# The Fourier transform along the channels on twice folded rows, in a fused linear attention and Fourier FFN kernel

## The chip, the cores and the metric

One NeuronCore of a Trainium2 chip. The metric is device time in microseconds of one execution. The kernel before took 1024.85 us, the median of 3 runs (1022.36 to 1027.26).

## What is computed

```python
# q, k, v: (8, 8, 576, 64); g_norm: (64)
kv = einsum('bhsd,bhse->bhde', k, v)
out = einsum('bhsd,bhde->bhse', q, kv)
rms = sqrt(mean(out * out, axis=-1, keepdims=True) + 1e-06)
x = (out / rms * g_norm)            # heads side by side: x is (8, 576, 512)
X = fft(fft(x, axis=1), axis=2)     # along the sequence, then along the channels
u = x + real(X)
un = (u - mean(u)) / sqrt(var(u) + 1e-06)
return u + maximum(un @ w_ch1, 0) @ w_ch2    # w_ch1: (512, 2048), w_ch2: (2048, 512)
```

w_ch1 and w_ch2 come as float64, and the kernel converts them itself.

## The kernel before, in words

**Number format.** Transforms and FFN run in fp32r. Each operand is split in a rounded high part and a low part, and each product is three matmuls (`passes`: high x high, high x low, low x high).

**First part, batch by batch (8 batches).** `plan_kv` (L574) makes k'v for a pair of heads; `plan_q` (L643) transposes q on TensorE; `plan_out` (L669) multiplies. A batch's 576 rows are handled as three tiles of 96 or 97 partitions, each holding a row p of the first half beside its mirror row of the second half, 512 channels each. `plan_y` and `plan_fold` scale x and fold it. Because the input is real, only sums (for the cosine) and differences (for the sine) of mirrored entries are needed, along the sequence and along the channels: L785 (VectorE) adds each channel d to channel 512 - d, for d = 1 to 256, taking the mirror row for the second term; L792 (GpSimd) then makes sum and difference of the two rows. ScalarE (L798) and GpSimd (L801) split the result `xe` into `xh` and `xl`. Column 0 has no partner; L779 (ScalarE) puts it into `x0`, and its own small transform (L1131) gives a constant per row that is added much later.

`plan_seq` transforms along the sequence: for each part (0 cosine, 1 sine) and each chunk `ch` of 128 folded channels, 9 matmuls of 290 columns (L816) make one bank `ps_f`, which ScalarE (L830) and VectorE (L834) split into the two tiles `pt`. `plan_chn` transforms along the channels: for each of the three row tiles and each part, 2 chunks x 3 passes = 6 matmuls with 96 or 97 weight columns (a slice of `pt`) and 258 moving columns of the table `cd` (L851). A ScalarE copy (L863) and two VectorE operations (L871) combine the two parts, and two additions (L883, L886; VectorE in batch 0, GpSimd later) add the result to x. `plan_turn` transposes the rows (L942) and splits them into `unTh` and `unTl` (L951, L954), blocks of 512 tokens for the FFN.

**FFN.** `ffn1` (L424) and `ffn2` (L442) take 512 moving columns each. Of the 16 slices of the hidden layer, 3 are done on a block as soon as it is complete (`plan_early`), between the batches' work; the others come after the first part, in `segs`, while the last weights are converted on VectorE (L359 to L369, L986, L995; later L1220).

**What sets the order.** `Plan` collects operations with an engine, a cost, a rank (batch and stage) and buffer rings, and plays them through: at each moment every engine takes the ready operation of lowest rank whose buffers are free. The order found is the program's order on each engine, fixed up to 95 us of the plan's clock (`PIN_UNTIL`). The table `SHIFT` moves the rank of single stages of single batches. FFN work has ranks over 1000 and so fills gaps. `plan_spare` gives TensorE 45 pairs of matmuls on a constant tile (`ps_s`, L494) of still higher rank, as filler. In batch 0 the DFT tables are loaded and split by `plan_dft` (L514 to L520).

## Time and profile before

| | |
|---|---|
| median of 3 runs | 1024.85 us |
| the profiled execution / its span | 1022.79 us / 1021.0 us |
| TensorE busy | 1002.3 us, 6070 matmuls |
| VectorE, ScalarE, GpSimd busy | 475.3, 324.8, 314.4 us |
| L851, the channel transform | 288 matmuls, 37.8 us busy |
| L816, the sequence transform | 288 matmuls |
| `ps_s`, filler | 90 matmuls |

The lines of the profile read `line engine operation out<-in shapes xcount | busy us, mean ns of one | idle before it, and what ended that`. Matmuls overlap, so the mean of one (285 ns for L851) is longer than the distance between two; distances are taken from windows and from the timeline. An fp32 matmul appears as two records, an fp32r matmul as one. PEld is TensorE's weight load.

### The profile page before, as it was taken

To read this page: it belongs to the slowest core of one execution; us is meant where nothing else is said; L and a number is where in the kernel's file an instruction comes from. 1 tells how busy PE (TensorE), PEld (TensorE's weight loads), DVE (VectorE), ACT (ScalarE), POOL (GpSimd) and SP (SyncE) were. 2 spreads that over 40 slices of the span, in tenths; PEclk is the share of its full clock that TensorE was granted. 3 is DMA by queue.
4 is the path that set the end of the run, shared out by engine and by line. 5 is a ranking of instruction groups with operands and counts; after the bars stand their busy time and mean duration, and the time that the engine had idled before them with its cause. 6 is when DMAs were issued, how large, how long until landed. Compare 5 with 4: busy or idle time off the path is not lost.

```text
span 1021.0 us, 15425 instructions
## 1 busy us (share of the span) xinstructions
PE 1002.3 (98%) x6070; PEld 844.0 (83%) x6070; DVE 475.3 (47%) x847; ACT 324.8 (32%) x657; POOL 314.4 (31%) x328
## 2 busy tenths in 40 slices
PE   5999999999999999999999999999999999999997
PEld 5898888889888888888888888888888888888886
DVE  4897656654788879997131313131221311311211
ACT  2666556554644434344221202121121120210110
POOL 0526768775675132235722303020020010100000
PEclk9999999999999999999999999999999999999999
DMA  9989778664346775645553514230320400400101
GB/s 250 212 230 282 181 209 258 162 170 131 137 163 213 268 253 191 236 129 170 161 179 86 180 59 150 82 125 0 141 67 1 165 21 1 165 0 1 42 1 42
DMA packets 109260, 140.74 MB, mean 138 GB/s; under 512 B 51854, under 2 KB 76482, under 8 KB 104580
## 3 DMA queue, kind: packets, MB, share of 16 engines
q1 hardware_dynamic: 105652, 132.28, 41.9%
q0 software_dynamic: 1920, 6.29, 1.9%
q10 hardware_dynamic: 1616, 1.18, 0.5%
q8 instruction: 48, 0.79, 0.3%
q14 instruction: 24, 0.20, 0.1%
HBM read 88.33 MB, written 51.40 MB: 137 GB/s over the span
## 4 chain that ended last, share of the span: by engine, by line
PE 97%; DMA 1%; ACT 0%; POOL 0%; DVE 0%; issue 0%; SPq 0%; DVEq 0%; POOLq 0%
PE ps_h L424 38%; PE acc L442 38%; PE ps_o L669 4%; PE ps_f L816 4%; PE ps_f L851 4%; PE ps_k L574 3%; PE ps_s L494 2%; PE ps_q L643 2%; PE ps_t L942 2%; DMA qt<-in_q_dram 1%; PE ps_w L383 1%; DMA vm<-in_v_dram 0%; POOL x L883 0%; ACT x L686 0%; DVE uu L1324 0%
## 5 line engine op out<-in xcount | busy, mean ns | idle before, releaser
L424 PE MATMUL ps_h<-unTh,w 128*128 128x512 f32 x1152 | 356.6, 391 | 1.2 <-ACT fq L647 1.2
L442 PE MATMUL acc<-w,hh 128*128 128x512 f32 x1152 | 345.5, 390 | 0.0
L437 DVE SCALAR_TENSOR_TENSOR hl<-ps_h,hh 128x512 fp32r<-128x512 f32 x144 | 99.1, 688 | 371.8 <-ACT hh L434 367.5
L442 PEld LDWEIGHTS acc<-w,hh 128*128 128x128 f32 x1152 | 215.1, 188 | 44.3
L424 PEld LDWEIGHTS ps_h<-unTh,w 128*128 128x128 f32 x1152 | 214.8, 188 | 44.8 <-ACT fq L647 1.4
L434 ACT ACTIVATE hh<-ps_h 128x512 fp32r<-128x512 f32 x144 | 85.8, 596 | 454.0 <-PE ps_h L424 439.2
L424 PE MATMUL ps_h<-unTl,w 128*128 128x512 f32 x576 | 224.3, 389 | 0.0
L442 PE MATMUL acc<-w,hl 128*128 128x512 f32 x576 | 213.5, 389 | 0.0
L424 PEld LDWEIGHTS ps_h<-unTl,w 128*128 128x128 f32 x576 | 108.1, 188 | 22.6
L442 PEld LDWEIGHTS acc<-w,hl 128*128 128x128 f32 x576 | 108.1, 188 | 22.6
L1271 POOL DMA_INDIRECT uu<-u_scr,rowidx x24 | 23.2, 968 | 285.1 <-DVE uu L1324 177.9
L709 POOL TENSOR_TENSOR x<-x,gb 96x512 f32<-96x512 f32 (+1 forms) x42 | 55.0, 1330 | 45.7 <-ACT x L686 40.3
L1290 POOL TENSOR_TENSOR uu<-uu,up 128x512 f32<-128x512 f32 x36 | 45.7, 1298 | 45.2 <-ACT up L1287 45.2
L1234 POOL TENSOR_TENSOR w<-wap,w 128x512 fp32r<-128x512 f32 x18 | 26.4, 1467 | 75.3 <-ACT w L1233 69.1
L669 PEld LDWEIGHTS ps_o<-kvt,fq 64*96 64x96 f32 (+1 forms) x864 | 40.9, 162 | 5.7 <-issue 4.0
L1324 DVE SCALAR_TENSOR_TENSOR uu<-acc,rs_yb,uu 128x512 f32<-128x512 f32 x36 | 25.2, 744 | 42.5 <-PE acc L442 42.5
L669 PE MATMUL ps_o<-kvt,fq 64*96 64x64 f32 (+1 forms) x864 | 44.4, 248 | 0.0
L696 DVE TENSOR_REDUCE ss<-ps_o 96x8 f32<-96x512 f32 (+1 forms) x48 | 32.0, 682 | 26.5 <-ACT ps_o L691 26.3
L792 POOL TENSOR_TENSOR xe<-ab 96x256 f32<-96x256 f32 (+1 forms) x46 | 38.0, 845 | 18.7 <-DVE ab L785 17.9
L816 PE MATMUL ps_f<-cs,xh 96*128 96x290 f32 (+1 forms) x192 | 39.0, 300 | 0.0
L1278 DVE BATCH_NORM_STATS2 bst<-uu 128x6 f32<-128x512 f32 x36 | 24.5, 687 | 29.0 <-DMA uu<-u_scr,rowidx 19.8
L851 PE MATMUL ps_f<-cd,pt 128*96 128x258 f32 (+1 forms) x288 | 37.8, 285 | 0.0
(114 smaller groups left out, 1022.4 us busy)
## 6 DMA issues: line engine op xcount, KB each, us to landing
raw<-in_moe_w_ch_dram SPq DMA_DIRECT2D x32, 512.0 KB
unT_scr<-unTh SPq DMA_DIRECT2D x9, 1024.0 KB
unT_scr<-unTl SPq DMA_DIRECT2D x9, 1024.0 KB
part_scr<-part SPq DMA_DIRECT2D x36, 256.0 KB
unTh<-unT_scr SPq DMA_DIRECT2D x9, 1024.0 KB
unTl<-unT_scr SPq DMA_DIRECT2D x9, 1024.0 KB
up<-part_scr SPq DMA_DIRECT2D x36, 256.0 KB
out_dram<-uu SPq DMA_DIRECT2D x36, 256.0 KB
```

What stands on the lines that cost most here:

```text
L424: nc.tensor.matmul(ps, w[c][:, kc * P : (kc + 1) * P], unT[a][:, kc, :], start=(idx == 0), stop=(idx == 3 * KC - 1),)
L434: nc.scalar.activation(hh, ps, AF.Relu)
L437: nc.vector.scalar_tensor_tensor(hl, ps, 0.0, hh.bitcast(F32), ALU.max, ALU.subtract)
L442: nc.tensor.matmul(acc, hpair[a][:, i * P : (i + 1) * P], w[c], start=(first and n == 0), stop=(last and n == 2),)
L574: nc.tensor.matmul(ps.t[s * D : (s + 1) * D, pr * D : (pr + 1) * D], km[:, s, j, :] if j < 4 else kr[:, h, :], vm[:, s, j, :] if j < 4 els ...
L669: nc.tensor.matmul(pss[s].t[:n, at : at + D], fqs[side].t[half, m, :n], kvt.t[half, m], start=True, stop=True,)
L696: nc.vector.tensor_reduce(ss.t[0][:n, :, t, s::2], pss[s].t[:n].rearrange("p (u m e) -> p u m e", u=2, e=D), AX.X, ALU.add,)
L709: nc.gpsimd.tensor_tensor(v_, v_, gb[:n].unsqueeze(1).to_broadcast([n, H, D]), ALU.mult)
L792: nc.gpsimd.tensor_tensor(o[:, s], a[:, 0], a[:, 1], ALU.subtract if s else ALU.add)
L816: nc.tensor.matmul(ps.t[:, :NS], xs[t].t[a][:n, part, ch * P : (ch + 1) * P], cs[:n, part, c, t, :], start=(idx == 0), stop=(idx == 8),)
L851: nc.tensor.matmul(ps.t[:n, :ND], pt.t[a][:, part, ch, offs[t] : offs[t] + n], cd[:, part, c, ch, :], start=(idx == 0), stop=(idx == 5),)
L1290: nc.gpsimd.tensor_tensor(us[j][i], us[j][i], part, ALU.add)
```

## The change

The spectrum along the channels has a symmetry that the kernel before did not use: with d' = 256 - d, cos(2 pi d' k / 512) is cos(2 pi d k / 512) for even k and its negative for odd k; for the sine it is the other way round. So after the sequence transform the two chunks of 128 channels are added and subtracted (row d with row 256 - d), and even columns k need only one of the results and odd columns the other. Each matmul of `plan_chn` still contracts 128 rows, but has 130 moving columns (even or odd ones) instead of 258; their number stays.

For this, `plan_fold` writes the second chunk in reverse order (three VectorE instructions instead of one). `plan_seq` handles both chunks of a part together: ScalarE copies the second bank to a new tile `far`, VectorE writes the sum into the second bank and the difference into the first, and both are split as before. Channel 128 is its own partner, and channel 256 is partner of column 0: in the cosine part the vector `paired` (1, and 0 for the last row) keeps them apart, one table row gets 1 in its odd columns, and the constant of column 256 goes into that of column 0, which a VectorE reduction (L834 of the new kernel) now adds instead of ScalarE. `plan_chn` writes even columns beside odd ones in a bank; copy and mix read them interleaved. The table's load and split are half as long (`plan_dft_d`).

The diff, cut:

```diff
 SHIFT = {
-    ("", "POOL", 20): 18,
-    ("chn", "ACT", -34): 54.5,
...
+    ("", "POOL", 30): 16.5,
+    ("chn", "DVE", -34): 14.5,
...
+    "x": 8, "raw": 2, "e2": 4, "wk": 2, "xhl": 3, "pt": 1, "two": 2, "far": 1,
...
+    NE = DH // 2 + 2
...
-    cd = cst.tile([P, 2, 2, 2, ND], F32R, name="cd")
+    cd = cst.tile([P, 2, 2, 2, NE], F32R, name="cd")
+    paired = cst.tile([P, 1], F32, name="paired")
+    nc.vector.tensor_scalar(paired, ident[:, P - 1 : P], -1.0, 1.0, ALU.mult, ALU.add)
...
+    def plan_dft_d(part, r):
+        raw = ring("x", one, [P, 2 * DM], "draw")
+        pad = op("POOL", 100, r, lambda: nc.gpsimd.memset(raw.t[:, ND : 2 * NE], 0.0), kv_loaded, [raw])
+        c = dma(132, r, lambda: nc.sync.dma_start(raw.t[:, :ND], dft_d[part, :, 0]), kv_loaded, [raw])
+        def by_parity():
+            return raw.t[:, : 2 * NE].rearrange("p (k e) -> p e k", e=2)
+        if part == 0:
+            c = op(
+                "DVE", 200, r,
+                lambda: nc.vector.tensor_scalar(
+                    by_parity()[:, 1], by_parity()[:, 1], ident[:, P - 1 : P], None, ALU.add
+                ),
+                [c, pad], [raw],
+            )
...
         def zero():
-            nc.scalar.activation(
-                x0[:n, t, b : b + 1], xv(0)[:, 0:1], AF.Identity, bias=xv(1)[:, 0:1]
-            )
+            nc.vector.tensor_reduce(x0[:n, t, b : b + 1], x.t[:n, :: DH], AX.X, ALU.add)
         def fold():
             xx = x.t[:n].rearrange("p (s d) -> p s d", s=2)
-            nc.vector.tensor_tensor(
-                two_of(ab), xx[:, :, 1 : DH + 1], xx[:, ::-1, DM - 1 : DH - 1 : -1], ALU.add
-            )
+            for at, lo, hi, step in ((0, 1, P + 1, 1), (P, DH - 1, P, -1), (DH - 1, DH, DH + 1, 1)):
+                width = (hi - lo) * step
+                nc.vector.tensor_tensor(
+                    two_of(ab)[:, :, at : at + width],
+                    xx[:, :, lo:hi:step],
+                    xx[:, ::-1, DM - lo : DM - hi : -step],
+                    ALU.add,
+                )
         def even(s):
             def go():
...
                 nc.gpsimd.tensor_tensor(o[:, s], a[:, 0], a[:, 1], ALU.subtract if s else ALU.add)
             return go
-        f = op("DVE", 690, r, fold, ms, [x, ab, xe], port=True)
-        z = op("ACT", 300, r, zero, ms + [i_x0], [x])
+        f = op("DVE", 860, r, fold, ms, [x, ab, xe], port=True)
+        z = op("DVE", 80, r, zero, ms + [i_x0], [x])
         e = [op("POOL", 830, r, even(s), [f], [ab, xe]) for s in range(2)]
         h = op("ACT", 640, r, lambda: nc.scalar.activation(xhl.t[0][:n], two_of(xe), AF.Copy), e, [xe, xhl])
...
-    def plan_seq(b, grp, xs, pt, dones):
-        part, ch = divmod(grp, 2)
-        ps = bank_buf("ps_f")
...
+    def plan_seq(b, part, xs, pt, dones):
+        pss, mms = [], []
         r = rank(b, SEQ)
-        a = op("PE", 1200, r, mm, dones + [dft["s", part]], [ps, pt] + xs)
-        a.dense = True
...
+        for ch in range(2):
+            ps = bank_buf("ps_f")
+            def mm(ch=ch, ps=ps):
...
+            a = op("PE", 1200, r, mm, dones + [dft["s", part]], [ps, pt] + xs)
+            a.dense = True
+            pss.append(ps)
+            mms.append(a)
+        far = ring("far", one, [P, NS], "far")
+        def out_():
+            nc.scalar.copy(far.t, pss[1].t[:, :NS])
+        def add():
+            p0, p1 = (ps.t[:, :NS] for ps in pss)
+            if part == 0:
+                nc.vector.scalar_tensor_tensor(p1, far.t, paired, p0, ALU.mult, ALU.add)
+            else:
+                nc.vector.tensor_tensor(p1, p0, far.t, ALU.add)
+        def sub():
+            p0 = pss[0].t[:, :NS]
+            if part == 0:
+                nc.vector.scalar_tensor_tensor(p0, p0, paired, far.t, ALU.mult, ALU.subtract)
+            else:
+                nc.vector.tensor_tensor(p0, p0, far.t, ALU.subtract)
+        f = op("ACT", 410, r - D2, out_, mms[1:], [pss[1], far])
+        e = op("DVE", 450, r - D2, add, [mms[0], f], [far] + pss)
+        o = op("DVE", 450, r - D2, sub, [e], [far, pss[0]])
+        done = []
+        for ps, parity, after in ((pss[1], part, e), (pss[0], 1 - part, o)):
...
+            h = op("ACT", 414, r - D2, high, [after], [ps, pt])
+            done.append(op("DVE", 450, r - D2, low, [h], [ps, pt]))
+        return done
     def plan_chn(b, t, x, pt, dones):
         n = rows[t]
...
             ps = bank_buf("ps_f")
             def mm(part=part, ps=ps):
-                idx = 0
-                for ch in range(2):
-                    for a, c in passes:
+                for e in range(2):
+                    for idx, (a, c) in enumerate(passes):
                         nc.tensor.matmul(
-                            ps.t[:n, :ND],
-                            pt.t[a][:, part, ch, offs[t] : offs[t] + n],
-                            cd[:, part, c, ch, :],
+                            ps.t[:n, e * NE : (e + 1) * NE],
+                            pt.t[a][:, part, e, offs[t] : offs[t] + n],
+                            cd[:, part, c, e, :],
                             start=(idx == 0),
-                            stop=(idx == 5),
+                            stop=(idx == 2),
                         )
-                        idx += 1
             pss.append(ps)
-            mms.append(op("PE", 720, r, mm, dones + [dft["d", part]], [ps, pt]))
+            mms.append(op("PE", 500, r, mm, dones + [dft["d", part]], [ps, pt]))
         me, pm = e2_buf("me"), e2_buf("pm")
-        c = op("ACT", 400, r - D2, lambda: nc.scalar.copy(me.t[:n, :W], pss[0].t[:n, :W]), mms[:1], [pss[0], me, pm])
+        def both(a):
+            return a[:n, : 2 * NE].rearrange("p (e k) -> p k e", e=2)[:, : ND // 2]
+        def single(a):
+            return a.rearrange("p (k e) -> p k e", e=2)
+        c = op(
+            "ACT", 400, r - D2,
+            lambda: nc.scalar.copy(single(me.t[:n, :ND]), both(pss[0].t)), mms[:1], [pss[0], me, pm],
+        )
         def pmv():
-            return pm.t[:n, : 2 * W].rearrange("p (s w) -> p s w", s=2)
+            return pm.t[:n, : 2 * ND].rearrange("p (s w) -> p s w", s=2)[:, :, :W]
         pms = []
         for s in range(2):
             def mix(s=s):
                 nc.vector.scalar_tensor_tensor(
-                    pmv()[:, s], pss[1].t[:n, :W], sgn_t[:n, s, 0:1], me.t[:n, :W], ALU.mult, ALU.add
+                    single(pm.t[:n, s * ND : (s + 1) * ND]), both(pss[1].t), sgn_t[:n, s, 0:1],
+                    single(me.t[:n, :ND]), ALU.mult, ALU.add,
                 )
             pms.append(op("DVE", 470, r - D2, mix, [c, mms[1], i_sgn], [pss[1], me, pm]))
...
             lows.append(l)
             zeros.append(z)
         pt = Buf("pt", lambda: [one.tile([P, 2, 2, NS], F32R, name=f"pt{i}") for i in range(2)])
-        pts = [plan_seq(b, grp, xhl, pt, lows) for grp in range(4)]
+        pts = sum((plan_seq(b, part, xhl, pt, lows) for part in range(2)), [])
         for t in range(3):
             plan_chn(b, t, xs[t], pt, pts)
         if b == 0:
```

In the rows of the program's order a number behind a name tells buffers apart. First, TensorE up to the first `ps_o` (batch 0; `ps_q` transposes of q, `ps_w` a mean over converted weights, `ps_k` of L574). Before:

```order
L643 MATMUL ps_q_154<-ident_72,qt_131 128x97 x4
L383 MATMUL ps_w_163<-wa_138,mean_t_83 128x128 x4
L643 MATMUL ps_q_173<-ident_72,qt_140 128x96 x4
L494 MATMUL ps_s_179<-still_108 128x512 x8
L643 MATMUL ps_q_201<-ident_72,qt_131 128x96 x4
L494 MATMUL ps_s_179<-still_108 128x512 x8
L643 MATMUL ps_q_221<-ident_72,qt_140 128x96 x4
L494 MATMUL ps_s_179<-still_108 128x512 x6
L574 MATMUL ps_k_239<-vm_114,km_171 64x64 x8
...
L494 MATMUL ps_s_179<-still_108 128x512 x4
L669 MATMUL ps_o_296<-kvt_240,fq_155 97x64
```

Now:

```order
L518 MATMUL ps_s_158<-still_110 128x512 x4
L629 MATMUL ps_k_166<-vm_116,km_136 64x64 x8
L629 MATMUL ps_k_166<-vr_131,kr_140 64x64 x2
L518 MATMUL ps_s_158<-still_110 128x512 x2
L404 MATMUL ps_w_188<-wa_148,mean_t_83 128x128 x4
L629 MATMUL ps_k_166<-vm_134,km_144 64x64 x8
...
L698 MATMUL ps_q_239<-ident_72,qt_161 128x97 x4
L518 MATMUL ps_s_158<-still_110 128x512 x2
L698 MATMUL ps_q_253<-ident_72,qt_180 128x96 x4
L518 MATMUL ps_s_158<-still_110 128x512 x4
L724 MATMUL ps_o_269<-kvt_167,fq_240 97x64
```

The four products of k and v of batch 0 now come first and the transposes of q behind them; 26 filler matmuls stood ahead of the first `ps_o`, and now 12.

On SyncE's queue, which issues most loads, from the first weights on (`raw` weights, `draw` DFT tables). Before:

```order
L349 DMA raw_127<-in_moe_w_ch2_dram 128x1024
L610 DMA qt_131<-in_q_dram 96x8x64
L624 DMA qt_131<-in_q_dram 1x8x64
L610 DMA qt_140<-in_q_dram 96x8x64
...
L483 DMA gb_104<-in_g_norm_dram 128x64
L553 DMA km_171<-in_k_dram 128x2x256
L562 DMA kr_185<-in_k_dram 64x8x64
...
L610 DMA qt_131<-in_q_dram 96x8x64
...
L349 DMA raw_252<-in_moe_w_ch1_dram 128x4x256
L349 DMA raw_274<-in_moe_w_ch2_dram 128x1024
```

Now:

```order
L370 DMA raw_129<-in_moe_w_ch2_dram 128x1024
L507 DMA gb_104<-in_g_norm_dram 128x64
L608 DMA km_136<-in_k_dram 128x2x256
L617 DMA kr_140<-in_k_dram 64x8x64
...
L665 DMA qt_161<-in_q_dram 96x8x64
L679 DMA qt_161<-in_q_dram 1x8x64
L665 DMA qt_180<-in_q_dram 96x8x64
...
L560 DMA draw_221<-in_dft_d_dram 128x258
...
L665 DMA qt_180<-in_q_dram 96x8x64
L541 DMA draw_259<-in_dft_s_dram 96x870
```

The loads of k moved ahead of all of q, and the second pair of weights behind the loads of batch 1.

On VectorE, around batch 0's sequence transform (`ss` row sums of the next batch, `ps_a` and `wp` weights). Before:

```order
L986 TENSOR_TENSOR ps_a_668<-ps_a_668,wp_669 128x512
L696 TENSOR_REDUCE ss_122<-ps_o_702 96x2x4
L834 TENSOR_TENSOR pt1_726<-ps_f_724,pt0_725 128x290
L696 TENSOR_REDUCE ss_122<-ps_o_703 96x2x4
L834 TENSOR_TENSOR pt1_726<-ps_f_744,pt0_725 128x290
L995 TENSOR_TENSOR w21_774<-ps_a_668,w21_774 128x512
L834 TENSOR_TENSOR pt1_726<-ps_f_761,pt0_725 128x290
```

Now:

```order
L1083 TENSOR_TENSOR ps_a_672<-ps_a_672,wp_673 128x512
L899 SCALAR_TENSOR_TENSOR ps_f_744<-far_771,paired_107,ps_f_727 128x290
L906 SCALAR_TENSOR_TENSOR ps_f_727<-ps_f_727,paired_107,far_771 128x290
L751 TENSOR_REDUCE ss_124<-ps_o_706 96x2x4
L919 TENSOR_TENSOR pt1_729<-ps_f_744,pt0_728 128x290
L919 TENSOR_TENSOR pt1_729<-ps_f_727,pt0_728 128x290
L901 TENSOR_TENSOR ps_f_778<-ps_f_760,far_806 128x290
L908 TENSOR_TENSOR ps_f_760<-ps_f_760,far_806 128x290
```

Four operations on the banks `ps_f` were added between the transform and its split.

More of the change, by code (lines that the diff above doesn't have):

```diff
@@ L523, in plan_dft @@
         dft[key, part] = c
+    def plan_dft_d(part, r):
[12 more added lines that the diff above has]
+            )
+        hi, lo = cd[:, part, 0], cd[:, part, 1]
+        c = op("ACT", 360, r, lambda: nc.scalar.activation(hi, by_parity(), AF.Copy), [c, pad], [raw])
+        dft["d", part] = op(
+            "DVE", 420, r,
+            lambda: nc.vector.tensor_tensor(lo, by_parity(), hi.bitcast(F32), ALU.subtract), [c], [raw],
+        )
     last_qkv = []
```

84 lines of the change are left out of this document (52 added, 32 removed).

## Prediction

> **What bounds the kernel now.** I read the page first, for the engines' shares, the slices and the granted clock.
>
> ```profile
> PE 1002.3 (98%) x6070; PEld 844.0 (83%) x6070; DVE 475.3 (47%) x847; ACT 324.8 (32%) x657; POOL 314.4 (31%) x328
> ...
> PE   5999999999999999999999999999999999999997
> ...
> DVE  4897656654788879997131313131221311311211
> ...
> PEclk9999999999999999999999999999999999999999
> ```
>
> TensorE is busy for 98% of the span, at full clock in every slice; VectorE has crowded slices in the first third. Next came the chain that ended last (by engine, by line) and TensorE's list of waits.
>
> ```profile
> PE 97%; DMA 1%; ACT 0%; POOL 0%; DVE 0%; issue 0%; SPq 0%; DVEq 0%; POOLq 0%
> PE ps_h L424 38%; PE acc L442 38%; PE ps_o L669 4%; PE ps_f L816 4%; PE ps_f L851 4%; PE ps_k L574 3%; PE ps_s L494 2%; PE ps_q L643 2%; PE ps_t L942 2%; DMA qt<-in_q_dram 1%; PE ps_w L383 1%; DMA vm<-in_v_dram 0%; POOL x L883 0%; ACT x L686 0%; DVE uu L1324 0%
> ```
>
> ```profile
> PE ps_q L643 <- DMA qt<-in_q_dram: 10.4, 1, 10.4
> PE ps_h L424 <- ACT fq L647: 1.2, 1, 1.2
> PE ps_k L574 <- DMA vm<-in_v_dram: 1.0, 1, 1.0
> PE ps_t L942 <- POOL x L883: 0.4, 1, 0.4
> ```
>
> So TensorE has one long wait, for the first load, and then 2.6 us of waits in all. But a full TensorE row isn't everywhere a bound. The matmuls `ps_s` are filler on a constant tile, and they sit in the first 90 us:
>
> ```profile
> L494 PE MATMUL ps_s<-still 128*128 128x512 f32 x90 | 25.3, 412 | 0.0
> ...
> L424 PE MATMUL ps_h<-unTl,w 128*128 128x512 f32 x576 | 224.3, 389 | 0.0
> ```
>
> Where filler runs, TensorE waits for others in truth. In TensorE's timeline the first FFN block begins at 77.20 us, and the second at 130.69, behind a wait:
>
> ```profile
> 77.20 0.63 PE L424 MATMUL ps_h<-unTh,w 128*128 128x512 f32 x2
> ...
> 130.69 0.73 PE L424 MATMUL ps_h<-unTh,w 128*128 128x512 f32 x2 [1.23 <-ACT fq L647]
> ```
>
> From 131 us on a backlog of FFN work is at hand and every nanosecond taken off TensorE counts; before that the chains of batches 0 and 1 set the pace. VectorE's windows show what limits these chains (busy time of each window), beside a later stage:
>
> ```profile
> 50.00:60.00 10.00, 9.36 (x17) 1.00 1.04 260
> 60.00:70.00 10.00, 9.46 (x17) 1.00 0.85 210
> ...
> 140.00:180.00 40.00, 25.07 (x47) 1.00 0.74 207
> ```
>
> VectorE is 94% busy from 50 to 70 us, and 63% from 140 to 180.
>
> **Part 1, the channel transform (L851, now L938).** The count stays: 8 batches x 3 tiles x 2 parts x 6 = 288 matmuls, each with its own weight load; the moving columns go from 258 to 130. What one costs in a row shows in TensorE's windows: one transform along the sequence (36 of 290 columns), two along the channels (36 of 258), 36 FFN matmuls (512).
>
> ```profile
> 102.77:107.58 4.81, 4.81 (x38) 1.00 1.09 226
> 285.37:289.67 4.30, 4.30 (x37) 1.00 0.17 65
> 314.67:318.97 4.30, 4.30 (x38) 1.00 0.45 117
> 335.44:343.72 8.28, 8.28 (x39) 1.00 0.83 342
> ```
>
> That is 4.81/36 = 134 ns, 4.30/36 = 119 ns and 8.28/36 = 230 ns: from 258 to 512 columns 0.437 ns a column. If only columns counted, 130 would cost 119 - 128 x 0.437 = 63 ns: the low bound. But the weight loads of this line run without a gap already (columns: TensorE, then weight loads):
>
> ```profile
> 285.30:289.70 4.40, 4.33 (x36) 4.23 (x36) 1.00 0.17 63
> ```
>
> The nearest row for loads of 96 weight columns behind short matmuls is `ps_o`; the nearest for 128 moving columns, but in plain fp32, is `ps_w`. Both end where the next row begins:
>
> ```profile
> 59.87 1.57 PE L669 MATMUL ps_o<-kvt,fq 64*96 64x64 f32 x32
> 61.37 0.84 PE L851 MATMUL ps_f<-cd,pt 128*97 128x258 f32 x5
> ...
> 67.39 1.16 PE L383 MATMUL ps_w<-wa,mean_t 128*128 128x128 f32 x8
> 68.39 0.83 PE L942 MATMUL ps_t<-ident,x 97*128 97x97 f32 x8
> ```
>
> `ps_o` runs its two halves of 64 rows side by side: 1.50/32 = 47 ns a record, so 94 ns for a load of 96 columns and its matmul in one half. `ps_w` takes 1.00/8 = 125 ns a record, and two records for each fp32 matmul (the order has 4, the trace 8): 250 ns, the high bound, if so narrow an fp32r matmul were run like plain fp32. I take 95 ns, from `ps_o`, since that row has the weight width of this line. In batches 2 to 7, behind 131 us, 216 matmuls then save 24 ns each: **-5.2 us**. The 72 of batches 0 and 1 save 1.7 us that turn into waiting, since their chains are held elsewhere: 0. The bounds for the 216: (119 - 63) x 216 = -12.1 us, and (250 - 119) x 216 = +28.3 us.
>
> The Trainium skill, "TensorE: Matmul & The Clock Gate", section "LDWEIGHTS (loading the stationary operand)", gives a load as its columns over 1.2 in ns, so an estimate of 80 ns for 96, and its section "Back-to-back issue gap" a sustained 81 ns for 128 moving columns with their loads. By that this part would be -8.2 us instead of -5.2. No row here shows such a matmul, and for 512 columns the same section says 131 ns where this trace has 230, so the rows keep the sum.
>
> **Part 2, VectorE and ScalarE.** Per batch, folding the spectrum adds two VectorE operations and one ScalarE copy for each of two parts; the row fold becomes three instructions instead of one; column 0 goes from ScalarE to a VectorE reduction. The prices (groups by line; 128x4 gives the fixed cost of a small one):
>
> ```profile
> L834 DVE TENSOR_TENSOR pt<-ps_f,pt 128x290 fp32r<-128x290 f32 x32 | 13.8, 454 | 9.4 <-ACT pt L830 9.2
> L871 DVE SCALAR_TENSOR_TENSOR pm<-ps_f,sgn_t,me 96x257 f32<-96x257 f32 x32 | 14.0, 475 | 7.0 <-POOL x L886 4.5 <-POOL xl L801 1.0 <-PE ps_f L851 0.5
> L954 DVE TENSOR_TENSOR unTl<-ps_t,unTh 128x4 fp32r<-128x4 f32 x8 | 1.3, 163 | 0.0
> L520 DVE TENSOR_TENSOR cd<-draw,cd 128x516 fp32r<-128x516 f32 x2 | 1.2, 650 | 0.0
> ...
> L830 ACT ACTIVATE pt<-ps_f 128x290 fp32r<-128x290 f32 x32 | 12.9, 415 | 15.0 <-PE ps_f L816 14.7
> L779 ACT ACTIVATE x<-x 96x1 f32<-96x1 f32 x16 | 4.7, 291 | 3.9 <-DVE x L774 3.8
> ```
>
> VectorE: 4 x 0.454 to 4 x 0.536 (L871's 475 ns scaled to 290 columns), so 1.8 to 2.1 us, and 3 x (2 + 1) x 0.163 = 1.5 us for the pieces: 3.3 to 3.6 us a batch. ScalarE: 2 x 0.415 - 3 x 0.291 = 0. The interleaved copy and mix in `plan_chn` keep their element counts; stride costs them nothing to a fifth of 475 ns more, I take nothing. Behind 131 us this lies under TensorE's backlog: 0. The next thing with a due time there is the last converted weights, ready at 368.1 + 0.7 us, beside the first FFN step on such weights at 376.84:
>
> ```profile
> 368.10 0.69 DVE L995 TENSOR_TENSOR w<-ps_a,w 128x512 fp32r<-128x512 f32 x1
> ...
> 376.84 0.62 PE L424 MATMUL ps_h<-unTh,w 128*128 128x512 f32 x2
> ```
>
> The pieces are used in the order made, so the last is due three steps after 376.84, some 3 x 12 x 0.23 = 8 us later: 16 us of slack, of which 5 us go to the earlier TensorE and 3.5 to the last batch's extra VectorE work. Cover stays. In batch 0 the extra 3.4 us stand on a 94% busy engine and are late by themselves: **+3.4**, less 2 x 0.33 = 0.7 for the halved `cd`. Batch 1 has VectorE time to spare behind 95 us: 0 to +3.5, I take 0.
>
> **Part 3, the new order of the first part.** Loads of batch 0's k and v are issued ahead of q, and weights 3 and 4 behind batch 1's k and v. Loads are a flow that fills its engines:
>
> ```profile
> DMA packets 16256, 10.04 MB, mean 251 GB/s; under 512 B 10427, under 2 KB 15547, under 8 KB 16253
> ...
> 22.11 0.69 PE L574 MATMUL ps_k<-vm,km 128*64 128x64 f32 x16
> 22.72 0.33 PE L574 MATMUL ps_k<-vr,kr 64*64 64x64 f32 x4
> 22.98 1.20 PE L494 MATMUL ps_s<-still 128*128 128x512 f32 x4
> 24.11 5.68 PE L669 MATMUL ps_o<-kvt,fq 64*97 64x64 f32 x128
> ```
>
> Up to the last k and v stand 1.05 MB of weights and 2.36 MB: 3.4 MB at 251 GB/s from 2 us on is 16 us, where `ps_k` ended at 23 before. Then two transposes of q, 1.4 us of filler, and `ps_o` begins at 19 to 21 instead of 24.11: -3 to -5 us, if q is there; the rest of q (to 4.9 MB, so 21.5 us) can take 1 to 2 of it back. Behind it stands the same work (86 filler matmuls up to the first FFN block in both orders), so I take the middle of both, -4 and +1.5: **-2.5**, with -4 and +4 as ends.
>
> **The sum.** -5.2 + 3.4 - 0.7 - 2.5 = -5.0 us. The profiled execution took 1022.79 us (span 1021.0), 2.06 below the median of the three runs; against the median, 1024.85 - 5.0 = **1019.8 us**, -0.5%. About 0.5%, 5.1 us, is what a measurement of this kernel can tell from no change, so the forecast stands on that edge.
>
> **The rivals.** *Only columns count* (63 ns): -12.1 in place of -5.2, so 1013 us. For it: `ps_k` above has 20 records between 22.11 and 22.98, so loads of 64 columns every 44 ns. Against it: the gapless weight loads. Chance 0.18.
> *Narrow matmuls lose the fp32r speed* (slower): at 250 ns L938 costs +28.3 us behind 131 us, and 72 x 131 ns = 9.4 more where the first two batches wait for it: 1053 to 1060 us. It decides from 119 ns upward. For it: no fp32r matmul under 258 columns is in this trace, and the short fp32 ones all come as two records. Against it: nothing shows that width matters to the type. Chance 0.14. The Trainium skill, "FP8 and Floating Point Precision", section "TensorE Precision Notes", says true fp32 takes four passes, an estimate of 4 x 63 = 252 ns here; the two records of 125 ns agree with it.
> *VectorE holds the first two batches* (slower or the same): batch 1 pays its 3.5 us too and the new order gives nothing back: -5.2 + 2.7 + 3.5 = +1.0, and +5.0 with the order's end of +4, so 1026 to 1030 us. It decides once the second FFN block begins more than 5 us behind 130.69. Chance 0.13.
> *The matmul stays at 119 ns*, held by its loads: 1025 us. Chance 0.05.
> The forecast, 85 to 105 ns and the order's ends within 2 us, has 0.50: 1015 to 1024 us.
>
> **How the numbers follow.** The range 1010 to 1036 holds all but the fp32 case and some tail of the first: 0.18 left out. Faster by over 0.5% (below 1019.7): 0.16 of the column case, 0.27 of the forecast, 0.02 of the rest: 0.45. Slower (above 1030.0): 0.14, 0.06 of the VectorE case at its end and 0.04 of waits not foreseen: 0.24. The rest, 0.31, is the same.
>
> **What would show it.** Windows of L938: 36 in 3.4 us means 95 ns; 2.3 the column case; 9 the fp32 case. The second FFN block's first matmul (130.69 before) shows parts 2 and 3. TensorE waits behind 131 us that add up to over 3 us would show that the backlog is not the cover I take it for, and the forecast would be wrong.

## The result, and the profile after

The changed kernel takes 1033.41 us (median of 6 runs, 1032.13 to 1038.19), the kernel before 1023.91 us in the same comparison (6 runs): a ratio of 1.0093, 95% interval 1.0069 to 1.0118. The forecast was 1019.8 us, 0.5% faster; it is 0.9% slower. The profiled execution took 1038.19 us, the longest of the six, with a span of 1036.4 us, 15.4 us over the span before; the medians are 9.5 us apart.

The page of the changed kernel (engines' shares, slices, the chain by engine):

```profile
PE 1010.5 (98%) x6070; PEld 846.9 (82%) x6070; DVE 504.0 (49%) x953; ACT 323.5 (31%) x649; POOL 306.9 (30%) x330
...
PE   5999889999999999999999999999999999999997
...
PEclk9999988999998999999999999999999999999999
...
PE 80%; DVE 8%; DMA 6%; issue 2%; POOL 2%; ACT 1%; SPq 0%; DVEq 0%; POOLq 0%; ACTq 0%
```

TensorE's share is still 98%, and it does less, yet it is busy for 8.2 us longer. The row to read is PEclk, the clock that TensorE was granted, a row of nines before: three slices now have a lower clock. The chain went from 97% TensorE to 80%. TensorE's waits:

```profile
PE ps_k L629 <- DMA kr<-in_k_dram: 8.5, 2, 7.2
PE ps_q L698 <- DMA qt<-in_q_dram: 2.6, 1, 2.6
PE ps_s L518 <- DVE still L511: 2.1, 1, 2.1
PE ps_k L629 <- DMA vm<-in_v_dram: 2.1, 1, 2.1
PE ps_f L938 <- ACT pt L916: 0.9, 1, 0.9
PE ps_f L938 <- DVE pt L919: 0.9, 1, 0.9
PE ps_t L1039 <- POOL x L980: 0.8, 2, 0.6
```

With some small ones they add up to 20.2 us, 13.0 before: 7.2 us more. What stands behind these pauses shows in windows of the stretch (last columns: granted clock, DMA share, GB/s):

```profile
104.00:108.00 4.00, 1.41 (x10) 0.91 (x9) 2.20 (x4) 3.56 (x10) 4.00 (x4) 1.00 0.89 196
108.00:112.00 4.00, 4.00 (x29) 2.87 (x27) 0.00 (x0) 0.98 (x2) 3.92 (x5) 0.61 0.59 136
...
148.00:150.00 2.00, 0.04 (x2) 0.07 (x3) 2.00 (x4) 0.32 (x1) 1.11 (x1) 0.96 1.09 368
150.00:162.00 12.00, 12.00 (x74) 10.96 (x75) 11.53 (x26) 5.08 (x12) 6.93 (x8) 0.50 0.47 94
...
304.00:307.00 3.00, 1.24 (x12) 0.96 (x11) 3.00 (x7) 2.14 (x5) 2.03 (x2) 0.98 0.00 0
307.00:317.00 10.00, 10.00 (x44) 8.25 (x44) 7.34 (x19) 1.00 (x2) 6.50 (x7) 0.50 0.18 58
```

A pause of 2.60 us at 107, one of 2.08 at 150, two of 0.87 and 0.88 at 305 to 306: behind each the clock stands at half, for 3.4, 13.7 and 10.2 us by the trace's clock records. In such a stretch TensorE is "busy" all the time, at half speed. Half of these 27.3 us, 13.7 us, is what they can cost. (The mean clock of 0.986 counts 2.5 us behind the last matmul too, which cost nothing.)

The row PEclk hides one stretch more. The first clock record of each trace, full clock, stands at 23.57 us in the changed kernel and at 13.62 us in the kernel before, and what lies ahead of it is shown as full. The lengths say otherwise; TensorE in the changed kernel, beside the same two forms in the kernel before, which the prediction shows at 22.11 and 22.98 us:

```profile
17.12 1.12 PE L629 MATMUL ps_k<-vm,km 128*64 128x64 f32 x16
...
22.11 1.20 PE L518 MATMUL ps_s<-still 128*128 128x512 f32 x2
...
24.70 2.96 PE L724 MATMUL ps_o<-kvt,fq 64*97 64x64 f32 x64
```

16 records of `ps_k` took 1.12 us instead of 0.69, and 2 of the filler `ps_s` as long as 4 before. Ahead of its first clock record TensorE was busy for 12.9 us, against 3.3 before; at half clock that is up to 4.8 us more lost.

The transform itself, in windows of its line (36 matmuls; TensorE, then weight loads):

```profile
63.96:67.06 3.10, 3.10 (x36) 3.10 (x36) 1.00 0.94 287
235.30:238.35 3.05, 3.05 (x36) 3.05 (x35) 1.00 0.22 86
```

That is 85 to 86 ns each, 119 before: 34 x 288 = 9.7 us saved. VectorE's new steps (groups by line):

```profile
L906 DVE SCALAR_TENSOR_TENSOR ps_f<-ps_f,paired,far 128x290 f32<-128x290 f32 x8 | 4.2, 525 | 0.0
L899 DVE SCALAR_TENSOR_TENSOR ps_f<-far,paired,ps_f 128x290 f32<-128x290 f32 x8 | 4.2, 522 | 1.5 <-ACT far L894 1.5
...
L901 DVE TENSOR_TENSOR ps_f<-ps_f,far 128x290 f32<-128x290 f32 x8 | 3.7, 460 | 1.2 <-ACT far L894 1.2
L908 DVE TENSOR_TENSOR ps_f<-ps_f,far 128x290 f32<-128x290 f32 x8 | 3.6, 456 | 0.0
```

The fold in pieces (L785 before, 23 instructions, 22.9 us):

```profile
L841 DVE TENSOR_TENSOR ab<-x 96x254 f32<-96x254 f32 (+5 forms) x69 | 45.0, 704 | 0.4 <-POOL xe L851 0.2
```

VectorE is busy for 504.0 - 475.3 = 28.7 us longer, 3.6 a batch. That is a net figure: the additions and subtractions take 15.7 us, the pieces 45.0 - 22.9 = 22.1 and the reduction for column 0 3.0, 40.8 us or 5.1 a batch, and other work of VectorE, weight conversion above all, took some 12 us less. The FFN blocks begin later; first matmuls of the first and the second block in the timeline:

```profile
82.54 0.63 PE L445 MATMUL ps_h<-unTh,w 128*128 128x512 f32 x2
...
139.23 0.73 PE L445 MATMUL ps_h<-unTh,w 128*128 128x512 f32 x2
```

They were at 77.20 and 130.69. The balance of TensorE's time in the two profiled executions: -9.7 (matmuls) + 7.2 (waits) + 13.7 (half clock behind pauses) + 4.8 (low clock at the start) = 16.0 us, beside the 15.4 measured. Both clock terms are upper bounds, since not all that runs at half clock takes twice as long.

### The profile page after: what moved, and what is told of

The parts are those of the page before. It is cut to its first block, busy times and chain, and to the rows that moved or that the text cites. A ratio compares the mean times of both kernels' runs of the same rounds, so it can differ in the third digit from the quotient of the medians.

```text
span 1036.4 us, 15533 instructions
## 1 busy us (share of the span) xinstructions
PE 1010.5 (98%) x6070; PEld 846.9 (82%) x6070; DVE 504.0 (49%) x953; ACT 323.5 (31%) x649; POOL 306.9 (30%) x330
## 3 DMA queue, kind: packets, MB, share of 16 engines
q10 hardware_dynamic: 1616, 1.18, 0.4%
## 4 chain that ended last, share of the span: by engine, by line
PE 80%; DVE 8%; DMA 6%; issue 2%; POOL 2%; ACT 1%; SPq 0%; DVEq 0%; POOLq 0%; ACTq 0%
PE ps_h L445 35%; PE acc L463 34%; PE ps_f L878 3%; PE ps_o L724 2%; DMA qt<-in_q_dram 2%; PE ps_k L629 2%; PE ps_f L938 2%; DVE ab L841 2%; DVE x L829 1%; DMA part_scr<-part 1%; DMA vm<-in_v_dram 1%; PE ps_t L1039 1%; DMA kr<-in_k_dram 1%; PE ps_s L518 1%; PE ps_q L698 1%
## 5 line engine op out<-in xcount | busy, mean ns | idle before, releaser
L841 DVE TENSOR_TENSOR ab<-x 96x254 f32<-96x254 f32 (+5 forms) x69 | 45.0, 704 | 0.4 <-POOL xe L851 0.2
L851 POOL TENSOR_TENSOR xe<-ab 96x256 f32<-96x256 f32 (+1 forms) x46 | 35.7, 795 | 29.5 <-DVE ab L841 17.8
L1331 POOL TENSOR_TENSOR w<-wap,w 128x512 fp32r<-128x512 f32 x18 | 23.3, 1293 | 70.5 <-ACT w L1330 70.5
L878 PE MATMUL ps_f<-cs,xh 96*128 96x290 f32 (+1 forms) x192 | 41.7, 311 | 0.0
## 6 DMA issues: line engine op xcount, KB each, us to landing
unT_scr<-unTh SPq DMA_DIRECT2D x9, 1024.0 KB
unT_scr<-unTl SPq DMA_DIRECT2D x9, 1024.0 KB
unTh<-unT_scr SPq DMA_DIRECT2D x9, 1024.0 KB
unTl<-unT_scr SPq DMA_DIRECT2D x9, 1024.0 KB
```

Of the source, the lines that this page charges most:

```text
L841: nc.vector.tensor_tensor(two_of(ab)[:, :, at : at + width], xx[:, :, lo:hi:step], xx[:, ::-1, DM - lo : DM - hi : -step], ALU.add,)
L851: nc.gpsimd.tensor_tensor(o[:, s], a[:, 0], a[:, 1], ALU.subtract if s else ALU.add)
L878: nc.tensor.matmul(ps.t[:, :NS], xs[t].t[a][:n, part, ch * P : (ch + 1) * P], cs[:n, part, c, t, :], start=(idx == 0), stop=(idx == 8),)
```

## The experiments

Three theories at first. A: the narrow transform is a gain; pauses under the new order, and half clock behind them, lose more. B: the longer VectorE chain is late under any order. C: the order table alone costs the time. "Old order" below is the order table of the kernel before. Ratios are to runs of the kernel before on the same chip.

**New arithmetic, old order** (1028.71 us, 1.0047, interval 1.0030 to 1.0065):

```diff
 SHIFT = {
-    ... the entries of the changed kernel
+    ... the entries of the kernel before
```

> The changed kernel with the order table of the kernel before: the narrow transform and its VectorE work alone. Theory A (the transform saves 34 ns on each of 288 matmuls, 9.7 us; what lost the time is pauses of TensorE under the new order, each with some us at half clock behind it): between 1014 and 1022 us, a mean granted clock of 0.995 or more, and no wait of 2 us on a load between 100 and 160 us. Theory B (the two more VectorE steps and the fold in pieces are late for TensorE whatever the order is): 1030 us or more, with waits on pt or on unTh and unTl, and the second FFN block's first matmul behind 134 us. Theory C (the order table alone is what costs): as A.

Neither. It is slower than before, so the new order isn't all; but the pauses are others (windows, then waits):

```profile
110.00:122.00 12.00, 11.46 (x171) 10.19 (x169) 9.43 (x24) 6.20 (x15) 5.20 (x6) 1.00 0.78 203
122.00:142.00 20.00, 17.48 (x136) 14.40 (x136) 11.04 (x21) 8.38 (x21) 16.68 (x20) 0.57 0.75 213
```

```profile
PE ps_t L1019 <- POOL x L960: 2.5, 2, 1.8
PE ps_q L678 <- DVE pt L899: 2.2, 1, 2.2
...
PE ps_f L918 <- ACT pt L896: 0.9, 1, 0.9
PE ps_f L918 <- DVE pt L899: 0.9, 1, 0.9
```

TensorE waits for batch 1's rows, then runs nearly 20 us at half clock, and the double pause ahead of batch 6's channel transform is there under this order as well.

**The new order on the kernel before** (1025.10 us, 1.0016, interval 1.0001 to 1.0030):

> The kernel before with the order table of the changed kernel, its transform left as it was. Theory C (the table alone costs the time): 1035 to 1045 us (the 9.7 us that the transform saves are missing), a mean clock near 0.986 and waits on qt and vm of 2 us and more. Theory B: within 5 us of 1024 us, clock 1.00. Theory A says that it depends on where the loads fall: slower than 1024 us if its trace shows a pause of 2 us with half clock behind it, and within 5 us of it if not.

The table alone costs next to nothing here, and with the old table the changed kernel is still slower than the kernel before; theory C, as the whole cause, falls. The trace of this run has one new pause, of 3.7 us, and half clock for some 4 us behind it, since the same table with other matmul costs yields another order. The next line is from its waits:

```profile
PE ps_q L663 <- DVE rs_y L754: 3.7, 1, 3.7
```

**Pauses by length**, in the kernel before:

```diff
+    def pause(ps, k):
+        nc.tensor.matmul(ps[:4, :4], zz[:, :4], zz[:, :4], start=True, stop=True)
+        nc.vector.tensor_reduce(zz[:, :k], ident.unsqueeze(1).to_broadcast([P, k, P]), AX.X, ALU.add)
+        nc.tensor.matmul(ps[:4, :4], zz[:, :4], zz[:, :4], start=True, stop=True)
```

> The kernel before with eight pauses of TensorE in the last part, where nothing else waits: a small matmul, a VectorE reduction of growing length on what it read, and a matmul that reads the result, at about 38 us from each other; the computed output is unchanged. Theory A: short pauses cost their own length and the clock stays at 1.00; from about 2 us on the clock stands at half for 4 to 11 us behind each, so the longest ones cost 4 to 8 us each and the run is 15 to 40 us longer. The rival (the low clock in the changed kernel comes with the hour or the chip, not with the pauses): 1.00 behind every pause, and the run longer by the sum of the pauses, about 12 us.

Pauses of 0.38, 0.64, 1.18 and 1.45 us left the clock alone. Of those of 1.71, 1.98, 2.39 and 2.38 us, the first three dropped it to half and the last did not (windows behind the pause of 2.39 us, which ended at 680.07, and behind that of 2.38, which ended at 887.90):

```profile
681.00:685.00 4.00, 4.00 (x12) 3.15 (x11) 1.44 (x7) 0.43 (x2) 0.00 (x0) 0.57 0.00 0
685.00:689.00 4.00, 4.00 (x19) 3.25 (x18) 0.69 (x1) 3.19 (x5) 2.84 (x3) 1.00 0.14 26
888.00:892.00 4.00, 4.00 (x19) 3.30 (x18) 0.29 (x1) 0.60 (x1) 0.00 (x0) 1.00 0.00 0
```

So among FFN matmuls a pause from 1.7 us on can halve the clock and need not, and it is back within 4 to 5 us, not 4 to 11. 1.7 us is no general border: in the first part of this same run a wait of 1.27 us for `vm`, up to 219.14 us and among `ps_k` and `ps_o`, had 3.4 us at half clock behind it. The run took 1051.98 us, 28 us over before (one run): 12.1 us of pauses, and half of four stretches of 3.4 us, 6.8 us of clock; the rest is not explained, one cause may be that TensorE's order was fixed for it throughout the last part.

**What brings the clock back**: pauses of 7.0 us (one 9.5), each followed by one kind of dummy matmul:

```diff
+        for _ in range(count):
+            if kind == "turn":
+                nc.tensor.transpose(ps[:, :96], ident[:96, :], ident[:96, :96])
+            elif kind == "heads":
+                nc.tensor.matmul(ps[:96, :64], ident[:64, :96], ident[:64, :64], start=True, stop=True)
+            else:
+                nc.tensor.matmul(
+                    ps[:cols, :moving], w[:rows_, :cols], x[:rows_, 0, :moving], start=True, stop=True
+                )
```

> The kernel before with eight long pauses (about 6.5 us) in the last part, each followed by 7 to 12 us of one kind of dummy matmul and then by the FFN's: none, 130 columns on 96 weight columns, 290 columns on 96 rows, 64x64 pieces, transposes, 512 columns, 258 columns, none. The computed output is unchanged. Theory A: every pause drops the clock to half; FFN matmuls and the 512 column ones bring it back in 4 us, the narrow, short and 96 row ones do not, so half clock then lasts as long as they do and 4 us more. The rival (the clock comes back by time alone, whatever runs): 4 us to 6 us at half behind each pause, the same for all kinds.

Windows, from the first matmul behind a pause (FFN; 130 columns, then the FFN behind them; 290 columns; 64x64 pieces):

```profile
606.47:611.40 4.93, 4.93 (x14) 3.91 (x15) 0.00 (x0) 0.00 (x0) 0.00 (x0) 0.56 0.00 0
654.10:673.40 19.30, 19.30 (x122) 19.27 (x123) 0.00 (x0) 0.00 (x0) 0.00 (x0) 0.50 0.00 1
673.46:676.00 2.54, 2.54 (x9) 2.01 (x9) 0.00 (x0) 0.00 (x0) 0.00 (x0) 0.56 0.00 0
722.60:727.20 4.60, 4.60 (x22) 4.57 (x23) 0.84 (x5) 3.14 (x5) 2.41 (x2) 0.53 0.03 4
727.20:734.00 6.80, 6.80 (x52) 6.80 (x51) 0.00 (x0) 0.00 (x0) 2.59 (x3) 1.00 0.56 151
780.80:829.00 48.20, 48.20 (x302) 48.15 (x302) 0.00 (x0) 0.00 (x0) 0.00 (x0) 0.50 0.00 1
```

At half clock the 130 column matmuls never brought it back in 19.3 us, nor the 64x64 pieces in 48.2 us; FFN matmuls, 290 columns on 96 rows, 258 columns, 512 columns and transposes did in some 4 to 6 us. My expectation had the wide and the transposes wrong. For this kernel it means that the form that the change brings in, and that of `ps_o`, did not end half clock in any stretch seen: it lasted until something denser had run for some microseconds. In the changed kernel that was the FFN block at 160.28 and that at 313.06 us; 18 matmuls of 290 columns, from 150.77 to 155.41, had been too few.

**The two worst pauses filled** (1026.05 us, 1.0019, interval 1.0002 to 1.0036), on new arithmetic and old order:

```diff
         def turn():
+            keep(ps.t, FILL_TURN.get((b, t, side), 0))
             for c in range(KC):
...
+                if part:
+                    keep(ps.t, FILL_CHN.get((b, t, 2), 0))
                 for e in range(2):
+                    if e and not part:
+                        keep(ps.t[:, 2 * NE :], FILL_CHN.get((b, t, 1), 0))
```

> The run with the new arithmetic and the old order table (1028.7 us), with dummy matmuls in its two worst pauses: 14 of 512 columns ahead of batch 1's first transposes (pauses of 0.67, 0.58 and 1.82 us at 122 to 126 us) and 11 shorter or longer ones ahead of batch 6's channel transform (0.87 and 0.88 us at 295 us). They do no useful work, and the transposes and matmuls behind them still wait for the same tiles. Theory A (the price is the half clock behind the pauses, 18 us and 10.5 us long there, so up to 14 us of TensorE work): 1013 to 1020 us, with the clock at 1.00 in both places. Theory B (the late tiles themselves are the price): 1027 to 1032 us, the fillers being no gain or a loss of up to 3 us.

Outside both: 2.7 us gained where A said 8.7 and more. The dummies held the clock at batch 6, but around 130 us another pause came up at once (1.45 us, for a bank that VectorE still read) and half clock with it; windows:

```profile
130.00:140.00 10.00, 9.74 (x80) 8.17 (x81) 5.00 (x13) 4.00 (x10) 8.32 (x13) 0.50 0.95 269
290.00:310.00 20.00, 19.15 (x127) 16.82 (x126) 17.77 (x42) 7.96 (x20) 14.55 (x16) 1.00 0.26 79
```

**Without the addition and subtraction** (1027.75 us, 1.0035, interval 1.0021 to 1.0048); it leaves out the folding of the spectrum:

```diff
-        far = ring("far", one, [P, NS], "far")
...
-        f = op("ACT", 410, r - D2, out_, mms[1:], [pss[1], far])
-        e = op("DVE", 450, r - D2, add, [mms[0], f], [far] + pss)
-        o = op("DVE", 450, r - D2, sub, [e], [far, pss[0]])
```

> The same run (new arithmetic, old order table) without the copy to far and the addition and subtraction of the two chunks: the banks are split at once, so the result is not the spectrum. Its TensorE work is unchanged. Theory B1 (the longer chain from the sequence to the channel transform brings the pauses): the pauses at 120 to 126 us and at 295 us are gone or below 0.5 us, the clock is 1.00 and the time 1010 to 1016 us. If they come from elsewhere (the fold in pieces, GpSimd's additions, loads): pauses of over 1 us and half clock stay, and the time stays over 1022 us.

Batch 6's pauses are gone, so the longer chain made those (the order behind it was found anew, too). But 32 VectorE operations and 16 ScalarE copies less gain only 1 us: pauses of 1.7, 1.4 and 1.3 us stand at 104 to 152 us, now for other tiles. Theory B falls as the main cause. Its waits:

```profile
PE ps_t L997 <- POOL x L938: 1.7, 1, 1.7
PE ps_q L678 <- DVE ss L731: 1.4, 1, 1.4
PE ps_f L858 <- POOL xl L840: 1.3, 1, 1.3
```

Each time one supplier is relieved, TensorE waits for the next. So theory D: behind 100 us, until the last batch is through, TensorE has no backlog.

**Narrow matmuls alone** (1025.45 us, 1.0021, interval 1.0000 to 1.0042), in the kernel before; it leaves out half of the columns in five of six products:

```diff
-                            ps.t[:n, :ND],
+                            ps.t[:n, : ND if idx == 0 else ND // 2 + 1],
...
-                            cd[:, part, c, ch, :],
+                            cd[:, part, c, ch, : ND if idx == 0 else ND // 2 + 1],
```

> The kernel before with five of each six channel transform matmuls cut from 258 to 130 columns, and nothing else: it leaves out products of 128 columns, so the result is not the spectrum. No work is added anywhere; TensorE has 240 x 34 ns = 8.2 us less to do. A backlog behind 131 us, as the prediction had it, gives 1024 less 72 x 5/6 x 0 and 216 x 5/6 x 34 ns = 6.1 us, so about 1018 us. Theory D gives 1021 us or more: what is saved before 320 us comes back as waits for the next tiles, and as half clock behind them.

As theory D had it: 8.2 us of TensorE work taken away, nothing added, and no gain. (Behind 95 us of the plan's clock the order came out a little differently: 135 of TensorE's 5293 instructions have changed places.) The mean clock of its 12 runs is 0.988 to 0.997. In the profiled execution, the fastest of them, TensorE's waits are 15.9 us instead of 13.0, and behind one of 0.9 us the clock stands at half for 6.8 us: 2.9 + 3.4 = 6.3 of the 8.2 us. Behind the first load the waits are spread over more suppliers than before:

```profile
PE ps_t L942 <- POOL x L883: 0.9, 1, 0.9
PE ps_o L1131 <- DVE x0h L1123: 0.8, 1, 0.8
PE ps_f L816 <- POOL xl L801: 0.6, 1, 0.6
PE ps_k L574 <- DMA vm<-in_v_dram: 0.6, 1, 0.6
```

**The changed kernel without one entry of its table** (1024.96 us, 1.0004, interval 0.9986 to 1.0022):

```diff
-    ("kv", "DMA", 30): -12,
```

> The changed kernel without the one entry of its order table that takes the k and v loads of batch 3 12 ranks ahead: q's load of batch 2 then stands 9 rows earlier in SP's queue. If that entry makes the 2.6 us wait for qt at 107 us: this wait is gone, the half clock behind it too (some 4 us at half), and the time is 1028 to 1031 us. If the queue is late whatever its order: the wait for qt stays over 1.5 us and the time at 1032 to 1036 us. In both cases batch 6's pauses at 305 us and the half clock behind them stay.

The load that TensorE waited for at 107 us was batch 3's second one of q; it moves up with batch 2's, from row 84 of SP's queue to row 76. The wait for `qt` is gone, and 8.5 us with it, more than either case had: its runs have clocks of 0.992 to 0.998 where the changed kernel had 0.986 to 0.990. The 8.5 us are not this one wait's. The 2.08 us wait for `vm` at 150 us and the 13.7 us at half clock behind it are gone as well, and at batch 6 one pause of 1.16 us is left, at 304 us, behind which the clock held. In exchange a channel transform at 119 us waits 1.83 us for `pt`, and 10.2 us at half clock follow. Windows of the two places:

```profile
118.00:132.00 14.00, 12.03 (x66) 11.65 (x65) 6.34 (x15) 5.16 (x14) 10.49 (x9) 0.63 0.37 104
300.00:320.00 20.00, 18.84 (x140) 16.80 (x139) 15.68 (x38) 10.21 (x26) 14.02 (x13) 1.00 0.27 83
```

**Batch 1's additions on VectorE** (1020.52 us, 0.9962, interval 0.9948 to 0.9976), on new arithmetic and old order, with batch 6's dummies:

```diff
-        eng = nc.vector if b == 0 else nc.gpsimd
+        eng = nc.vector if b < 2 else nc.gpsimd
```

> New arithmetic and old order table, with batch 1's two additions per row tile on VectorE, as batch 0's are, instead of GpSimd (which was busy 10.00 of 10 us from 120 to 130 us while TensorE waited 3.1 us for them), and the 11 dummy matmuls ahead of batch 6's channel transform kept; the other dummies are gone. Theory D (behind 100 us TensorE has no backlog: it stands at the batches' supply, here GpSimd, and each pause there also costs some 10 us at half clock): the pauses at 122 to 130 us are below 1 us in sum, the clock stays at 1.00 there, and the time is 1015 to 1021 us. If another engine is as late, a pause of over 1 us stands within 10 us of the old place, half clock follows it, and the time stays at 1024 to 1029 us.

Its time is in the range of D, and it is faster than both kernels. D's other signs did not come up: the pause at 125 us is not gone (1.8 us, now for VectorE's addition), and in the profiled execution half clock follows it to 142 us. What moved here against the run with the old order is the additions and batch 6's dummies together. Three of 12 runs had a clock of 0.996, and took 1016.7 to 1017.3 us.

**The same move in the kernel before** (1024.92 us, 1.0001, interval 0.9987 to 1.0015):

> The kernel before with batch 1's two additions per row tile on VectorE instead of GpSimd, and its wide transform. If the 3.7 us that the run with both gained over the kernel before come from the narrow transform, once its tiles are in time: 1022 to 1026 us here, no change. If they come from the moved additions alone: 1019 to 1021 us.

No change: in the wide kernel the moved additions gain nothing. But this run lacks batch 6's dummies as well, and without them the run with the narrow transform is not clear of the kernel before either (the last run, 0.9990). What gained 3.7 us is the narrow transform, the moved additions and the dummies together; the share of the narrow transform is not shown.

**The same run with that pause filled** (1026.49 us, 1.0023, interval 1.0012 to 1.0034):

```diff
-FILL_TURN = {}
+FILL_TURN = {(1, 0, 0): 3, (1, 0, 1): 2, (1, 1, 0): 5}
```

> The run with batch 1's additions on VectorE (1020.5 us, clock 0.990 to 0.996 over its runs), with 10 dummy matmuls of 512 columns ahead of batch 1's first transposes, where 2.3 us of pauses stood at 122 to 126 us. The order of the work is otherwise the same and the transposes still wait for the same rows, so what changes is the clock. If half clock behind the pause is a price of its own: the clock is 1.00 from 120 to 145 us, 0.996 or more over the run, and the median is 1015 to 1018 us, below both kernels. If the low clock costs nothing (TensorE waits for tiles there anyway): 1020 to 1022 us.

It does not decide what it was meant to: the dummies changed the order that the scheduler chose behind them, and two pauses of 2.6 and 2.7 us for VectorE's additions stood at 130 to 134 us instead.

**Without batch 6's dummies** (1024.16 us, 0.9990, interval 0.9967 to 1.0012):

```diff
-FILL_CHN = {(6, 0, 1): 7, (6, 0, 2): 4}
+FILL_CHN = {}
```

> The run with batch 1's additions on VectorE (1020.5 us) without its 11 dummy matmuls ahead of batch 6's channel transform. Up to 290 us the instructions stand in the same order on all engines, and from there on in nearly the same, so this tells the price of the clock there by itself: in the run with new arithmetic and old order two pauses of 0.87 and 0.88 us stood at this place, with 10.5 us at half clock behind them; the dummies (1.9 us) had filled them. If half clock is a price of its own: pauses of 1.5 to 2 us come back, half clock for about 10 us behind them, a mean clock lower by 0.005, and the time is 1024 to 1026 us, 4 to 5 us more. If only the pauses count: 1020 to 1021 us, since the dummies took as long as the pauses.

This is the cleanest comparison, and it speaks for a price of half clock by itself: 3.6 us by the medians. The two runs were on different chips; by their ratios, 0.9962 and 0.9990, it is 2.9 us, and the intervals just overlap. Half of the 6.8 us that its trace has at half clock there is 3.4 us. Windows of the run with the dummies, then of that without:

```profile
291.00:300.00 9.00, 8.62 (x63) 7.26 (x62) 5.97 (x13) 2.73 (x7) 4.92 (x5) 1.00 0.13 44
```

```profile
291.00:300.00 9.00, 8.20 (x41) 7.38 (x42) 2.54 (x6) 1.49 (x4) 1.99 (x2) 0.62 0.01 2
```

Its own 12 runs fit: the two with a clock of 0.996 took 1016.8 and 1017.1 us, as long as the three with that clock in the run with the dummies (1016.7 to 1017.3), the six with 0.987 or 0.988 from 1024.0 to 1025.9. Beside the run with the old order (1.0047) it differs in the moved additions alone: with the narrow transform these are worth some 5 us.

## Why the prediction was wrong

**Part 1, right in its mechanism, undersized.** 85 to 86 ns instead of 95: 34 ns saved, not 24; "only columns count", "loses the fp32r speed" and "stays at 119 ns" are out. The Trainium skill's 80 to 81 ns ("TensorE: Matmul & The Clock Gate", sections "LDWEIGHTS (loading the stationary operand)" and "Back-to-back issue gap"), kept out of the sum, was nearer. The step that failed is the one behind it: "From 131 us on a backlog of FFN work is at hand and every nanosecond taken off TensorE counts". With 8.2 us taken off and nothing added, the time did not fall. I read a backlog from 98% busy and 2.6 us of waits. I now read them as a balance: while batches come in, TensorE and its suppliers finish close to each other, and the FFN slices at hand are only the three of each complete block. What was saved there turned into waits (2.9 us more) and half clock behind one of them (3.4 us). Whether another order would have kept some of it was not tried with the narrow matmuls alone.

**Pauses had no price in the sum.** I took a wait to cost its length. Several here had 3.4 to 13.7 us at half clock behind them, so up to 1.7 to 6.8 us more, and no stretch of the narrow form ended it. Over all 105 runs of the kernel before in these comparisons the median is 1022.6 us at a clock of 1.000 (24 runs), 1024.7 at 0.998 (44) and 1027.7 at 0.994 (12). The chance of 0.04 for "waits not foreseen" was the case that came.

**Part 2, one price too low, cover wrong.** 3.3 to 3.6 us of VectorE a batch were forecast. The net of 3.6 meets that by luck: the additions cost 2.0 us a batch as forecast (1.8 to 2.1), but the pieces and the reduction 25.1 / 8 = 3.1 instead of 1.5, and other work came out shorter. "Behind 131 us this lies under TensorE's backlog: 0" and "Cover stays" failed: the longer chain makes batch 6's double pause. Leaving its additions out is worth 1 us, batch 6's dummies some 3, so this is part of the loss and not most of it.

**Part 3, -2.5 forecast.** The first `ps_o` came at 24.70 us, not 19 to 21. The last rows of k (`kr`) were there at 13.85 us, so the loads were about as early as forecast; what failed is that I took TensorE's work behind them at full speed. Up to 23.57 us it ran at a low clock, and at the lengths of the kernel before the same work would have ended some 5 us earlier (an estimate from the rows). With the same first part of the order, the runs with the new order on the kernel before and without the one entry had full clock from 17.85 and 18.94 us, and their first `ps_o` at 22.52 and 22.77. The larger mistake is that I priced only the head of the load queue. The entry that takes batch 3's k and v, issued from 37 to 62 us, ahead of batch 2's costs 8.5 us, with all that it moves.

**The rival "VectorE holds the first two batches"** was nearest: its sign (the second block 8.5 us late, where it named 5) came up, and its 1026 to 1030 us lack the half clock and the load. The other sign named, waits behind 131 us of over 3 us, came up too (5.6 us). Of the fp32 rival, which is out, the upper end was added up wrongly: 1053 + 9.4 is 1062, not 1060.

Shown are: no gain from TensorE's saving alone in nearly the same order, the cost of the one entry as a whole, the chain as cause of batch 6's pauses, and, at the edge of the noise, the price of half clock at one place. Only argued: the split of the 15.4 us, which is a balance of one execution and not a sum of tested causes. Open is what exactly decides whether a pause halves the clock; one of 2.39 us did and one of 2.38 did not.

The Trainium skill, same page, section "Part 1: The HAM clock gate", would explain this by activity windows of about 3.4 us that run freely, so that the effect of a pause depends on where it falls. Two things in the traces agree: the return within 4 to 6 us of dense work, and that every stretch at half clock that ended in a trace lasted a whole multiple of 3.41 us (3.41 to 54.61). Laid on steps of 3.41 us counted from the clock records, 2.10 us of the pause of 2.39 fall into one step, and of that of 2.38 only 1.72 and 0.66. The page's rule that an idle window of about 3.4 us is needed does not agree, since 1.71 us were enough among FFN matmuls, and 0.89 to 1.27 us among narrower ones.

## What to carry to other kernels

An engine at 98% may be bound or may merely be in balance with its suppliers. Before a saving on it is counted, look for the stretch where its next work always lies ready; elsewhere, ask who comes last once it is earlier, and relieve that one with it, as the additions of batch 1 here. Count a pause of TensorE of a microsecond or two as a risk of some microseconds at half clock behind it, up to the next dense block, and read the granted clock beside the busy time. At the start of a trace compare the lengths of equal matmuls instead, since the clock row has nothing to show ahead of its first record.

## What the runs showed of the hardware

At half clock a 130 column matmul on 96 weight columns took 158 ns (19.3 us for 122), at full clock 85. A stream of these, or of 64x64 pieces, with no gap in TensorE's row, left the clock at half for 19.3 and 48.2 us, until the run of them ended. Full clock was held through 36 of the 130 column matmuls in a row in the changed kernel (3.1 us), and through 128 records of 64x64 pieces in the kernel before (5.6 us, from 24.11); whether a longer run of either would lose it was not tried.

The shortest single pauses with half clock behind them stood among narrow matmuls and transposes: 0.89 us (narrow matmuls alone), 1.08 and 1.52 us (the moved additions in the kernel before), 1.27 us (pauses by length).
